# Loads of the first block over two DMA queues in another order, and a swap of two matmul groups, in a fused state-space and feed-forward kernel

## The chip, the cores and the metric

The kernel runs on one core of a Trainium2 chip. The core has five engines that run at once and meet through semaphores: TensorE (PE, matmuls; PEld is its weight load), VectorE (DVE), ScalarE (ACT), GpSimd (POOL) and SyncE (SP). The last one only issues DMAs here. ACT can issue DMAs too, on a queue of its own. The metric is device time in microseconds, and it is better when smaller.

## The reference

The input x has 2048 tokens of 512 features in bfloat16. It is normalised, and the output is x plus two branches of the normalised xn:

```python
xn = _layernorm(x, axis=-1)
return x + _A_ref(xn, Lambda_re, ..., Dskip) + _B_ref(xn, w_gate, w_up, w_down)

# A: a diagonal complex recurrence over the tokens
dt = exp(log_dt);  Lam_bar = exp(dt * Lam);  B_bar = ((Lam_bar - 1) / Lam)[:, None] * Bmat
h = Lam_bar * h + (xn @ B_bar.T)[t]                # for each token t
y = 2 * (h @ Cmat.T).real + xn * Dskip
# B: a gated feed-forward layer, 512 -> 1376 -> 512
(_gelu(xn @ w_gate) * (xn @ w_up)) @ w_down
```

The three vectors log_dt, Lambda_re and Lambda_im have 512 entries each; w_gate and w_up are 512 x 1376.

## The kernel before

**Tiling.** The tokens are cut into four blocks of 512, and a block into four token tiles of 128 rows: X[0] to X[15], 128 KB each. The feed-forward width is cut into 11 tiles of 128 columns (the last has 96). The contraction over 512 features goes in four steps of 128, called k = 0 to 3 here ("step 3" is k = 3).

**The first block.** Blocks 1 to 3 are normalised first and then multiplied. Block 0 starts before its statistics are known. Its token tiles are only centred (the mean is subtracted: lines 956 to 968 for tiles 0 and 1, line 951 for tiles 2 and 3), transposed by TensorE (`cent_T`, L684), evicted from PSUM by ACT (L689), and multiplied with the weights; the scale 1/sigma comes in when the sums are evicted (`GT_evac`, L721 and L724). `GT_k` (L701) is one matmul of contraction step k for token tile j and width part u: 256 columns wide when it takes gate or up alone, 512 when it takes both. `ks(k, j, [w])` issues the two parts u = 0, 1; w = 0 is gate, w = 1 is up. So the early matmuls can begin as soon as one token tile and 128 rows of w_gate are there. Line 936 keeps TensorE busy until then. After the early groups `GT_mm` (L712) does what is left of the first seven width tiles of block 0.

**The loads.** Each DMA is an operation of the queue that issues it. SP issues X[0]; then for k = 0 to 3 rows 128k to 128k+127 of the first 512 columns of w_gate and then of w_up (`ld_wk`, L488, 128 KB each), with X[3] ahead of k = 3; then the middle 384 columns of both (chunk 1, `ld_w`, L493), and the last 480 (chunk 2). ACT issues X[1], then the three parameter vectors as rows of a small tile PROW (`load_par`, L510), then X[2]. `tr_par` (L515) transposes PROW with a DMA on SP. From then on SP issues, in the order of the program: `TR(0)` (four DMA transposes of the normalised tiles of block 0, L736), the load of block 1, the transposing loads of B, the row Dskip, the load of block 2, `TR(1)`, and so on.

**What sets the order.** The operations are recorded with their reads and writes, from which the waits follow. Those of TensorE and SP run in the order in which they are recorded. Those of VectorE, ACT and POOL are put in order by a planner that reckons with costs of its own (a DMA holds its queue for 500 ns, unless told otherwise), save where `order_behind` ties one operation behind another; `ch` chains VectorE's early work in this way: mean and centring of tiles 0 and 1, statistics of tile 0, statistics and centring of tile 2, statistics of tile 1, statistics and centring of tile 3, then the normalising of tiles 0 and 1. `GATE["par"]` chains what ACT issues, and ties the mean of tile 1 (`mean1`, L956, on ACT) behind the last of it.

**Behind the first block** TensorE does the rest of the feed-forward layer of block 0 (`GU`, L843 and L817), the input products of the recurrence of blocks 0 and 1 (`BU`, L749; BU(1) begins with the first two token tiles of block 1, so with the first two transposes of TR(1)), then `GU`, `BU` and the down product with the state product (`DN`, L885) block by block. VectorE runs the recurrence (L774 to L803).

Of the kernel before, what the change touches and what calls it, by code (L numbers as in the profile page):

```python
# [361 lines left out]
def d_act(n, ptr=0): return 190.0 + 0.833 * n + 90.0 * ptr  # L362
# [3 lines left out]
def build(nc, ins, out):  # L366
    with ExitStack() as es:
        E = es.enter_context
        S = Sched(nc, es)
# [9 lines left out]
        WG = A.alloc("WG", [KD, F], BF16)  # L379
        WU = A.alloc("WU", [KD, F], BF16)  # L380
# [4 lines left out]
        WGc = [Buf("WGc%d" % i, "sbx", 10 * i, 10 * i + 1) for i in range(KD + 2)]  # L385
        WUc = [Buf("WUc%d" % i, "sbx", 100 + 10 * i, 101 + 10 * i) for i in range(KD + 2)]
# [34 lines left out]
        PROW = A.alloc("PROW", [128], BF16)  # L421
        PROW16 = Buf("PROW16", "sb", PROW.lo, PROW.hi, PROW.ap[0:16, :])
        PROWq = [Buf("PROW%d" % q, "prow", q, q + 1) for q in range(3)]
# [46 lines left out]
        GATE = {"before_gelu": [], "nh": 0}  # L470
        SCR = A.alloc("SCR", [1], F32)
        half = V(lambda e: e.memset(HALF.ap, 0.5), D_TINY, [], [HALF], "half")
# [10 lines left out]
                X_all.ap[:, 4 * b:4 * b + 4, :], x2[512 * b:512 * (b + 1), :].rearrange("(j p) d -> p j d", p=128)),  # L483
                512 * 1024, writes=X[4 * b:4 * b + 4], tag="ld_x%d" % b)

        def ld_wk(W, Wc, src, k):
            f0, f1 = FC[0]
            return S.dma(lambda e: e.dma_start(W.ap[:, k, f0:f1], src[128 * k:128 * (k + 1), f0:f1]),  # L488
                         256 * (f1 - f0), writes=[Wc[k]], tag="ld_w")

        def ld_w(W, Wc, src, n):
            f0, f1 = FC[n]
            return S.dma(lambda e: e.dma_start(W.ap[:, :, f0:f1], src[:, f0:f1].rearrange("(k p) f -> p k f", p=128)),  # L493
                         1024 * (f1 - f0), writes=[Wc[KD + n - 1]], tag="ld_w")

        def ld_x0(j, queue="sync", after=()):
            return S.dma(lambda e, j=j: e.dma_start(X[j].ap, x2[128 * j:128 * (j + 1), :]), 128 * 1024, writes=[X[j]], tag="ld_x0", queue=queue, after=after)  # L497
        ld_x0(0)
        GATE["par"] = S.order_behind(ld_x0(1, "scalar", [wrm]), GATE["table"])
        for k in range(KD):  # L500
            if k == 3:
                ld_x0(k)
            ld_wk(WG, WGc, ins["B_w_gate"], k)
            ld_wk(WU, WUc, ins["B_w_up"], k)
        ld_w(WG, WGc, ins["B_w_gate"], 1)
        ld_w(WU, WUc, ins["B_w_up"], 1)

        def load_par():
            for q, nm in enumerate(("A_log_dt", "A_Lambda_re", "A_Lambda_im")):
                GATE["par"] = S.order_behind(S.dma(lambda e, q=q, nm=nm: e.dma_start(PROW.ap[4 * q:4 * q + 4, :], ins[nm].rearrange("(s p) -> s p", p=128)),  # L510
                      1024, writes=[PROWq[q]], tag="ld_" + nm, queue="scalar", after=[half]), GATE["par"])
            GATE["par"] = S.order_behind(ld_x0(2, "scalar"), GATE["par"])

        def tr_par():
            S.dma(lambda e: e.dma_start_transpose(PAR.ap.rearrange("p q t -> p (q t)").unsqueeze(1), PROW16.ap), 4096,  # L515
# [162 lines left out]
        def cent_T(j, k0, k1, bank):  # L678
            pt = PS[bank].bitcast(BF16)[:, 0:128 * (k1 - k0)]

            def f(e):
                ins_ = None
                for k in range(k0, k1):
                    ins_ = e.transpose(pt[:, 128 * (k - k0):128 * (k - k0 + 1)], XN[j].ap[:, 128 * k:128 * (k + 1)], IDN.ap)  # L684
                return ins_
            PE(f, 56.0 * (k1 - k0), [XNp[j][k0 > 0] if j < 2 else XN[j], IDN], [BANK[bank]], "T0")
            dst, src = XC_all.ap[:, k0:k1, 128 * j:128 * (j + 1)], pt.rearrange("p (q t) -> p q t", t=128)
            w = XCs[j] if k1 - k0 == KD else [XCs[j][k0 > 0]]
            GATE["evTA"] = ACT(lambda e: e.activation(dst, src, ACTF.Copy), d_act(128 * (k1 - k0)), [BANK[bank]], w, "evT")  # L689
# [6 lines left out]
        def GT_k(k, j, u, ws, first=False):  # L696
            f0, f1 = FR[u]
            w = f1 - f0
            bank = acc(j, u)
            dst = PS[bank][:, w * ws[0]:w * (ws[-1] + 1)].rearrange("p (w f) -> p w f", w=len(ws))  # L700
            PE(lambda e: e.matmul(dst, XCd(j, k), WGU[:, ws[0]:ws[-1] + 1, k, f0:f1], start=first, stop=k == KD - 1, skip_group_check=True),  # L701
               d_pe([w * len(ws)]), [(WGc, WUc)[w_][k] for w_ in ws] + [XCs[j][k > 0]] + ([] if first else [BANK[bank]]), [BANK[bank]], "GK")
# [247 lines left out]
        def sub(j):  # L950
            return V(lambda e: e.tensor_scalar(XN[j].ap, X[j].ap, MVt[0][j].ap[:, 0:1], None, ALU.subtract),
                     d_dve_ts4x(512), [X[j], MVt[0][j]], [XN[j]], "sub")
        load_par()
        load_W()
        tr_par()
# [17 lines left out]
        def ks(k, j, w_, first=False):  # L973
            for u in range(2):
                GT_k(k, j, u, w_, first)
        cent_T(1, 0, 1, 6)
        ks(0, 0, [0], True)
        cent_T(1, 1, 4, 7)
        ks(0, 0, [1])
        ks(0, 1, [0], True)  # L980
        ks(0, 1, [1])
        ch(*stats(0, 0))
        for w_ in range(2):
# [75 lines left out]
def bass_parallel_sum__ssm_conv_s5__geglu_ffn__prompt_kernel(  # L1059
    nc: bass.Bass,  # L1060
    A_x: bass.AP,
    A_Lambda_re: bass.AP,
    A_Lambda_im: bass.AP,
    A_B_re: bass.AP,
    A_B_im: bass.AP,
    A_C_re: bass.AP,
    A_C_im: bass.AP,
    A_log_dt: bass.AP,
    A_Dskip: bass.AP,
    B_x: bass.AP,  # L1070
    B_w_gate: bass.AP,
    B_w_up: bass.AP,
    B_w_down: bass.AP,
    out: bass.AP,
):
    ins = {
        "A_x": A_x, "A_Lambda_re": A_Lambda_re, "A_Lambda_im": A_Lambda_im,
        "A_B_re": A_B_re, "A_B_im": A_B_im, "A_C_re": A_C_re, "A_C_im": A_C_im,
        "A_log_dt": A_log_dt, "A_Dskip": A_Dskip,
        "B_w_gate": B_w_gate, "B_w_up": B_w_up, "B_w_down": B_w_down,  # L1080
    }
    build(nc, ins, out)
# [28 lines left out]
```

## Time and profile before

| what | value |
|---|---|
| time, median of 3 runs | 177.05 us (176.91 to 177.43) |
| profiled execution | 177.26 us |
| its span | 175.9 us |
| busy: PE, DVE, ACT, POOL | 172.8, 159.7, 95.8, 10.7 us |
| granted TensorE clock | 1.00 |
| HBM read, written | 6.46 MB, 2.10 MB |

The span is what the profiler records, from the first instruction to the last; the profiled execution's time is 1.36 us longer. The loads of the start, from the trace (issue, and landing, which is issue plus the time to landing), in us from the start of the span:

| load | queue | issue | landing |
|---|---|---|---|
| X[0] | SP | 0.74 | 2.84 |
| X[1] | ACT | 1.00 | 3.2 |
| gate 0, up 0 | SP | 1.20, 1.66 | 3.6, 4.56 |
| gate 1, up 1 | SP | 2.13, 2.60 | 5.43, 6.27 |
| X[2] | ACT | 2.66 | 6.06 |
| gate 2, up 2 | SP | 3.08, 3.56 | 6.48, 7.16 |
| X[3] | SP | 4.03 | 7.5 |
| gate 3, up 3 | SP | 4.50, 4.98 | 8.1, 8.78 |
| chunk 1: gate, up | SP | 5.47, 5.95 | 10.27, 11.95 |
| chunk 2: gate, up | SP | 6.50, 7.04 | 13.3, 14.6 |
| parameter transpose | SP | 7.82 | 15.0 |

The three rows were issued by ACT at 1.42, 2.03 and 2.32; their landing is not in the trace.

### The profile page before, as it was taken

The numbers are of one execution on the slowest core, as the hardware profiler recorded it, in microseconds if no ns is written. First come the engines' busy times: TensorE is split into PE (matmuls) and PEld (weight loads), VectorE is DVE, ScalarE is ACT, GpSimd is POOL, SyncE is SP. The second block draws the span as 40 slices with busy tenths as digits, with TensorE's granted clock in tenths as the row PEclk, the third lists the DMA queues.
The fourth block names the chain that finished last, engine by engine and source line by source line (L and its number), as shares of the span: only waits on it lengthen the run. The fifth ranks groups of instructions, "written<-read, shape, count | busy, mean of one in ns | idle before, by whom it ended". The sixth has DMA issues, their size and how long they took to land.

```text
span 175.9 us, 2549 instructions
## 1 busy us (share of the span) xinstructions
PE 172.8 (98%) x903; PEld 85.4 (49%) x903; DVE 159.7 (91%) x279; ACT 95.8 (54%) x187; POOL 10.7 (6%) x24
## 2 busy tenths in 40 slices
PE   7999999999999999999999999999999999999995
PEld 2645664744544444444644444444464444444454
DVE  6797999987999989889899999989999899999941
ACT  5367668999766899383676793000667970000000
POOL 3132120211000000002200000000000000000000
DMA  5999989975899000002015000002004000000311
GB/s 144 281 322 154 216 136 203 174 132 114 162 270 270 11 0 2 0 30 75 18 33 112 5 0 4 0 0 89 30 0 34 0 0 0 0 0 4 119 62 60
DMA packets 32421, 14.36 MB, mean 82 GB/s; under 512 B 23737, under 2 KB 32409, under 8 KB 32409
## 3 DMA queue, kind: packets, MB, share of 16 engines
q1 hardware_dynamic: 31952, 13.84, 36.9%
q10 hardware_dynamic: 456, 0.36, 0.6%
q8 instruction: 7, 0.11, 0.3%
q14 instruction: 6, 0.04, 0.1%
HBM read 6.46 MB, written 2.10 MB: 49 GB/s over the span
## 4 chain that ended last, share of the span: by engine, by line
PE 95%; DMA 2%; SPq 1%; issue 0%; DVE 0%
PE PS L885 37%; PE PS L843 32%; PE PS L749 16%; PE PS L712 4%; PE PS L817 3%; PE PS L701 2%; DMA arena<-in_B_w_up_dram 2%; SPq L488 1%; PE PS L684 0%; SPq L497 0%; DVE arena L903 0%
## 5 line engine op out<-in xcount | busy, mean ns | idle before, releaser
L885 PE MATMUL PS<-arena 128*128 128x512 bf16 (+3 forms) x323 | 66.2, 366 | 0.0
L843 PE MATMUL PS<-arena 128*128 128x512 bf16 (+1 forms) x272 | 58.1, 373 | 0.0
L885 PEld LDWEIGHTS PS<-arena 128*128 128x128 bf16 (+1 forms) x323 | 30.8, 98 | 35.2
L843 PEld LDWEIGHTS PS<-arena 128*128 128x128 bf16 x272 | 26.5, 98 | 29.5
L787 DVE TENSOR_TENSOR_SCAN arena<-arena 128x512 bf16<-128x512 f32 x32 | 38.9, 1256 | 0.0
L859 ACT ACTIVATE arena<-PS 128x512 bf16<-128x512 f32 x33 | 19.8, 599 | 26.2 <-DVE arena L903 16.7
L749 PE MATMUL PS<-arena 128*128 128x512 bf16 (+1 forms) x144 | 28.3, 355 | 0.1
L863 ACT ACTIVATE arena<-PS 128x512 bf16<-128x512 f32 x33 | 19.8, 599 | 5.4 <-PE PS L843 5.4
L749 PEld LDWEIGHTS PS<-arena 128*128 128x128 bf16 x144 | 14.0, 98 | 13.7 <-DMA arena<-arena 0.6
L877 ACT ACTIVATE PS<-arena 128x512 f32<-128x512 bf16 (+2 forms) x17 | 9.6, 582 | 19.7 <-DVE arena L903 19.0
L758 ACT ACTIVATE arena<-PS 128x512 bf16<-128x512 f32 x32 | 17.6, 597 | 1.6 <-PE PS L749 1.6
L903 DVE TENSOR_TENSOR arena<-PS,arena 128x512 bf16<-128x512 f32 (+2 forms) x17 | 10.9, 654 | 6.4 <-PE PS L885 6.4
L865 DVE TENSOR_TENSOR arena<-arena 128x512 bf16<-128x512 bf16 x33 | 13.2, 419 | 2.1 <-ACT arena L863 2.0
L776 DVE TENSOR_TENSOR arena<-arena 128x4096 bf16<-128x4096 bf16 (+1 forms) x5 | 9.2, 1859 | 0.4 <-ACT arena L611 0.4
L799 DVE TENSOR_TENSOR arena<-arena 128x4096 bf16<-128x4096 bf16 x4 | 9.2, 2291 | 0.1
L774 DVE TENSOR_TENSOR arena<-arena 128x4096 bf16<-128x4096 bf16 (+1 forms) x5 | 9.2, 1861 | 0.0
L800 DVE TENSOR_TENSOR arena<-arena 128x4096 bf16<-128x4096 bf16 x4 | 9.1, 2287 | 0.0
L615 DVE BATCH_NORM_STATS2 arena<-arena 128x6 f32<-128x512 bf16 x12 | 7.8, 685 | 0.9 <-DMA arena<-in_A_x_dram 0.7
L721 ACT ACTIVATE arena<-PS,arena 128x256 bf16<-128x256 f32 (+1 forms) x16 | 6.5, 450 | 3.3 <-DVE arena L621 1.5
L712 PE MATMUL PS<-arena 128*128 128x512 bf16 (+1 forms) x40 | 7.1, 336 | 0.0
L701 PE MATMUL PS<-arena 128*128 128x256 bf16 (+1 forms) x36 | 6.2, 308 | 0.2 <-DMA arena<-in_B_w_up_dram 0.2
L724 DVE SCALAR_TENSOR_TENSOR arena<-PS,arena 128x256 bf16<-128x256 f32 (+1 forms) x16 | 6.2, 444 | 0.0
(95 smaller groups left out, 124.2 us busy)
## 6 DMA issues: line engine op xcount, KB each, us to landing
out_dram<-arena SPq DMA_DIRECT2D x15, 128.0 KB, 1.7
arena<-in_A_x_dram SPq DMA_DIRECT2D x3, 512.0 KB, 6.3
arena<-in_B_w_down_dram SPq DMA_DIRECT2D x1, 1280.0 KB, 8.8
arena<-in_B_w_gate_dram SPq DMA_DIRECT2D x4, 128.0 KB, 3.4
arena<-in_B_w_up_dram SPq DMA_DIRECT2D x4, 128.0 KB, 3.6
arena<-in_B_w_gate_dram SPq DMA_DIRECT2D x1, 480.0 KB, 6.8
arena<-in_B_w_up_dram SPq DMA_DIRECT2D x1, 480.0 KB, 7.6
arena<-arena SPq DMA_TRANSPOSE x25, 3.3
```

Source lines behind the costliest of these rows:

```text
L701: PE(lambda e: e.matmul(dst, XCd(j, k), WGU[:, ws[0]:ws[-1] + 1, k, f0:f1], start=first, stop=k == KD - 1, skip_group_check=True), d_pe([w ...
L712: ins_ = e.matmul(dst, XCd(j, k), WGU[:, :, k, f0:f1], start=(k == 0), stop=(k == KD - 1))
L749: ins_ = e.matmul(PS[bank][:, 128 * j0:128 * j1], BBT[c][dk].ap[:, 128 * s:128 * (s + 1)], XNT[b].ap[:, dk, 128 * j0:128 * j1], start=(dk ...
L758: GATE["evBu"] = ACT(lambda e, bank=bank, k3=k3, s=s, c=c: e.activation(SSc[k3][s][c].ap, PS[bank][:, :], ACTF.Copy), d_act(512), [BANK[ba ...
L787: V(lambda e, g=g, rb=rb, init=init: e.tensor_tensor_scan(g.ap, rb, g.ap, init, ALU.mult, ALU.add), d_dve_scan(512), [g, PA[RRr]] + ([CARc ...
L843: ins_ = e.matmul(PS[bank][0:m, c0:c1], W.ap[:, dk, 128 * ft:128 * ft + m], XNT[b].ap[:, dk, c0:c1], start=(dk == 0), stop=(dk == KD - 1))
L859: GATE["last_gelu"] = ACT(lambda e, bg=bg, kk=kk, m=m: e.activation(GG[kk].ap[0:m, :], PS[bg][0:m, :], ACTF.Gelu_apprx_tanh), d_act(512), ...
L863: ACT(lambda e, bu=bu, kk=kk, m=m: e.activation(UPB[kk].ap[0:m, :], PS[bu][0:m, :], ACTF.Copy), d_act(512), [BANK[bu]], [UPB[kk]], "evU")
L865: V(lambda e, kk=kk, m=m, ft=ft, k2=k2: e.tensor_tensor(HTt[k2][ft].ap[0:m, :], GG[kk].ap[0:m, :], UPB[kk].ap[0:m, :], ALU.mult), d_dve_tt ...
L877: ACT(lambda e: e.activation(PS[bank][:, c0:c1], X[tt].ap[:, c0:c1], ACTF.Copy), d_act(c1 - c0), [X[tt]], [BANK[bank]], "seed")
L885: ins_ = e.matmul(PS[bank][:, c0:c1], l_[:, 128 * j:128 * (j + 1)], r_[:, c0:c1], start=False, stop=last and n == len(ops) - 1, skip_group ...
L903: V(lambda e: e.tensor_tensor(OUTB[ko].ap[:, c0:c1], PS[bank][:, c0:c1], XD[tt].ap[:, c0:c1], ALU.add), d_dve_1x(c1 - c0), [BANK[bank], XD ...
```

## The change

The up rows of steps 0, 1 and 2 go from SP's queue to ACT's. X[2] stands behind the up rows of step 1 on ACT's queue, ahead of those of step 2. The three parameter rows go from ACT's queue to SP's, behind the up rows of step 3 and ahead of chunk 1; SP still issues chunk 1, chunk 2 and the parameter transpose in this order. `mean1` on ACT is now tied behind the up rows of step 2. In TensorE's order the gate matmuls of tile 1 in step 0 go ahead of the up matmuls of tile 0.

```diff
-        def ld_wk(W, Wc, src, k):
+        def ld_wk(W, Wc, src, k, queue="sync"):
             f0, f1 = FC[0]
             return S.dma(lambda e: e.dma_start(W.ap[:, k, f0:f1], src[128 * k:128 * (k + 1), f0:f1]),
-                         256 * (f1 - f0), writes=[Wc[k]], tag="ld_w")
+                         256 * (f1 - f0), writes=[Wc[k]], tag="ld_w", queue=queue)
...
             if k == 3:
                 ld_x0(k)
             ld_wk(WG, WGc, ins["B_w_gate"], k)
-            ld_wk(WU, WUc, ins["B_w_up"], k)
-        ld_w(WG, WGc, ins["B_w_gate"], 1)
-        ld_w(WU, WUc, ins["B_w_up"], 1)
+            if k < 3:
+                GATE["par"] = S.order_behind(ld_wk(WU, WUc, ins["B_w_up"], k, "scalar"), GATE["par"])
+            else:
+                ld_wk(WU, WUc, ins["B_w_up"], k)
+            if k == 1:
+                GATE["par"] = S.order_behind(ld_x0(2, "scalar"), GATE["par"])
 
         def load_par():
             for q, nm in enumerate(("A_log_dt", "A_Lambda_re", "A_Lambda_im")):
-                GATE["par"] = S.order_behind(S.dma(lambda e, q=q, nm=nm: e.dma_start(PROW.ap[4 * q:4 * q + 4, :], ins[nm].rearrange("(s p) -> s p", p=128)),
-                      1024, writes=[PROWq[q]], tag="ld_" + nm, queue="scalar", after=[half]), GATE["par"])
-            GATE["par"] = S.order_behind(ld_x0(2, "scalar"), GATE["par"])
+                S.dma(lambda e, q=q, nm=nm: e.dma_start(PROW.ap[4 * q:4 * q + 4, :], ins[nm].rearrange("(s p) -> s p", p=128)),
+                      1024, writes=[PROWq[q]], tag="ld_" + nm)
+            ld_w(WG, WGc, ins["B_w_gate"], 1)
+            ld_w(WU, WUc, ins["B_w_up"], 1)
...
         cent_T(1, 1, 4, 7)
+        ks(0, 1, [0], True)
         ks(0, 0, [1])
-        ks(0, 1, [0], True)
         ks(0, 1, [1])
```

## The prediction

> **What bounds the kernel now.** I read four views, from the whole to the spot. First the page: busy times (its part 1) and the chain that ended last (its part 4).
>
> ```profile
> PE 172.8 (98%) x903; PEld 85.4 (49%) x903; DVE 159.7 (91%) x279; ACT 95.8 (54%) x187; POOL 10.7 (6%) x24
> ...
> PE 95%; DMA 2%; SPq 1%; issue 0%; DVE 0%
> ```
>
> TensorE is the bound, with 95% of the chain. What is not matmul lies at the start, so the second view is that chain in order of time (start us, length, what).
>
> ```profile
> 2.60 3.67 DMA arena<-in_B_w_up_dram
> 6.28 0.05 issue
> 6.32 1.26 PE PS L701 x10
> ...
> 31.52 0.12 issue
> 31.64 7.11 PE PS L749 x48
> ```
>
> TensorE waits at two places that end last. One is at 6.3: the load of up rows, step 1, issued at 2.60 by SP, lands at 6.27. The matmul before it started at 5.84 and costs 0.11 (the spacing of the 256-wide ones), so 6.32 - 5.95 = 0.37 us are lost. The other is at 31.6, where BU(1) begins; the matmul before it started at 31.14 and costs 0.22, so 0.28 is lost. From 31.64 to the end TensorE runs without a gap. The third view, the timeline, says what feeds the two places (start us, length, engine, line, what; in brackets the idle time before and its releaser).
>
> ```profile
> 2.66 0.36 ACTq L497 DMA_DIRECT2D arena<-in_A_x_dram  x1
> 6.11 0.69 DVE L615 BATCH_NORM_STATS2 arena<-arena 128x6 f32<-128x512 bf16 x1 [0.74 <-DMA arena<-in_A_x_dram]
> 7.06 0.35 DVE L951 TENSOR_SCALAR arena<-arena 128x512 bf16<-128x512 bf16 x1
> 7.46 0.23 PEld L684 LDWEIGHTS PS<-arena 128*128 128x128 bf16 x4 [0.16 <-DVE arena L951]
> 7.82 1.99 SPq L515 DMA_TRANSPOSE arena<-arena  x1
> 9.82 0.73 DVE L634 TENSOR_SCALAR arena<-arena 128x512 bf16<-128x512 bf16 x2
> 10.27 5.15 SPq L736 DMA_TRANSPOSE arena<-arena  x4
> 24.17 6.34 SPq L736 DMA_TRANSPOSE arena<-arena  x4
> 31.61 6.64 PEld L749 LDWEIGHTS PS<-arena 128*128 128x128 bf16 x48 [0.58 <-DMA arena<-arena]
> ```
>
> Token tile 2 (X2) is issued by ACT at 2.66 and lands 3.4 later, at 6.06. VectorE has waited 0.74 for it, and then works without a gap (statistics, L951, statistics of two more tiles) until it normalises token tile 0 at 9.82. That lets SP start TR(0) at 10.27, and from there SP issues one DMA behind the other (loads, the transposes of B) to TR(1) at 24.17. The second transpose of TR(1), issued at 26.62, lands 4.9 later, at 31.5, and TensorE stands at 31.36 waiting for it. So the wait at 6.3 lies on the path of TensorE alone, and a second path, X2 - VectorE - TR(0) - SP - TR(1), arrives 0.28 later at 31.6. **What ends last there is the landing of X2, not that of up.** A microsecond that TensorE wins before 31.6 shows in the time only as far as this path moves too.
>
> The fourth view is the DMA queues, in a table by stages (engines' busy times, granted clock, DMA share, GB/s) and in the window 4.5 to 5.0 (q1 is SP's queue, q10 is ACT's).
>
> ```profile
> 2.00:3.00 1.00, 1.00 (x4) 0.43 (x3) 0.45 (x2) 0.23 (x2) 0.37 (x2) 1.00 0.97 329
> 3.00:4.50 1.50, 1.36 (x10) 0.43 (x9) 1.24 (x7) 1.21 (x4) 0.00 (x0) 1.00 0.75 197
> 4.50:6.00 1.50, 1.50 (x16) 1.14 (x15) 0.83 (x3) 0.92 (x3) 0.00 (x0) 1.00 1.00 338
> ...
> q10 hardware_dynamic: 97, 0.09, 54.0%
> q1 hardware_dynamic: 90, 0.09, 49.1%
> ```
>
> The engines are full at 330 GB/s, but between 3.0 and 4.5 they get work for only 197: SP issues one 128 KB load each 0.47 us, and ACT issues three rows of 1 KB. When both queues hold data, each gets half.
>
> **The change, part by part.** SP loses three up loads and gains three rows; ACT issues X1, up 0, up 1, X2, up 2 instead of X1, three rows, X2. An ACT issue of 128 KB takes 0.37 and 0.04 between, so I expect them at 1.00, 1.42, 1.83, 2.24, 2.65. SP issues X0, gate 0, 1, 2, X3, gate 3, up 3 by 4.0, then the three rows, the four chunks, and the parameter transpose (L515).
>
> *Up of step 1.* On ACT's queue at half of 330 GB/s a load takes 0.79. X1 had all packets by 3.0, so up 0 is through at 3.8, up 1 at 4.6, X2 at 5.35, up 2 at 6.15. From last packet to landing the rows of before show 0.25 (X1) to 0.5. Up 1 lands at 4.9 to 5.1, before its use at 5.95. The wait of 0.37 goes.
>
> *TensorE's order.* Gate of tile 1 now needs the eviction of that tile's first transpose, which ended at 4.93; the matmul in that place started at 4.86. Cost 0.07 to 0.31 (the nearest wait for an operand there, 0.31 at 4.37); I take 0.12, a semaphore's delay behind 4.93. Mean1 on ACT stands behind five issues, which end at 3.03 as before, or at 3.30 if each takes the 0.43 of SP's: 0 to 0.1. All of it is covered: without its wait TensorE would reach the transposes of tile 2 at 7.43 - 0.37 + 0.12 + 0.1 = 7.28 at worst, and L951 frees them at 7.41. If that cover were gone, 0.2 would stay before 11 us and be swallowed at 31.6, where TensorE has 0.28.
>
> *X2, the term that counts.* Issued 0.42 earlier, but behind two more loads on its own queue. Below: every 0.1 that it lands earlier moves VectorE, TR(0) and TR(1) by 0.1, down to 5.36, where VectorE is free: at most a gain of 0.74 - 0.04 = 0.70. Above: it is the eighth load by issue; the eighth to land before was at 6.48 and the ninth at 7.16, so a loss of 0.42 to 1.10. I take the queue sum, 5.35, and the 0.6 that X2 itself showed between its bulk (5.4 at the latest) and landing: 5.95, a gain of 0.1. It lies nearest because it uses the measured half share.
>
> *Rows and the parameter transpose.* An issue of a row took 0.27 to 0.57 on ACT, so SP is at L515 between 7.4 and 8.2, as before (7.82) within 0.4. It also waits for the rows, which now go behind 12 loads: 12 x 131 KB at 330 GB/s, from 2.0 on, are through at 6.8, and the landing is 0.25 to 0.5 later, say 7.2. From below nothing is won (L515's result was waited for at 15.1 by POOL behind all loads). From above: the twelfth load landed at 8.78 before; L515 would then start at 8.9, end at 10.9, and TR(0) begin 0.66 late. I take nothing, since TR(0) has 0.46 behind L515's end at 9.81.
>
> *The rest.* X3 comes earlier by 1.4 in issue and was used 0.84 after landing: nothing. Chunk 1 landed at 10.27 and 11.95 and is used at 12.73: up to 0.4 later costs nothing. PROW's clearing by POOL ended at 1.22, long before SP issues the rows.
>
> **Sum.** -0.1 at 31.6, and TensorE, which stood there at 31.36, is in time. The profiled execution took 177.26 (span 175.9 and 1.36 around it), 0.21 above the median of 177.05. So 177.16 for it, and 176.95 for the median.
>
> The Trainium skill ("DMA: Bandwidth & Descriptors", section "Issuing engines are not separate DMA queues") says that starting DMAs from several engines saves only the sequencer's time, as all run on the same 16 engines. The trace agrees for 4.5 to 6.0 (338 GB/s, share 1.00) and shows sequencer time to be saved from 3.0 to 4.5 (share 0.75). By the rule alone X2 would win what the idle quarter of 1.5 us gives and lose its extra load ahead, near nothing. Its section "Queues, rings and completion order" has each engine take turns between queues, which 54.0% and 49.1% bear out.
>
> **The rivals.**
> *X2 lands early (faster).* For it: the idle quarter of 3.0 to 4.5 is worth 0.25 x 1.5 = 0.38, and X2 is issued 0.42 earlier; with its old 3.4 to landing it is there at 5.64, with X0's 2.1 before VectorE is free. If it lands before 5.53, the time falls by 0.53 to 0.70: 176.4. Against it: two more loads ahead of it, and that L515 must start by 7.7 (it holds SP for 1.99, and TR(0) would have to begin at 9.74).
> *X2 lands late (slower).* ACT's queue carries three weight loads, and when SP's queue gets more than half, X2 falls from the seventh to the ninth place. It decides from a landing of 6.6; between that and 7.16 it costs 0.53 to 1.10: 177.85. For it: gate 2, issued after X2 before, landed only 0.42 after it. Against: equal shares. The skill's rule named above speaks for this one.
> *Rows land late (slower).* A new wait of SP at L515, as worked out: from rows at 8.7 on; 177.05 + 0.66 = 177.7. For it: the rows now stand behind 0.9 MB in their own queue; against: SP's old weight queue is three loads shorter there.
> *The wait is only renamed* is my forecast itself: up no longer holds TensorE, L951 does.
>
> **How the numbers follow.** The bound of what a measurement tells is 0.3%, 0.53 us. Renamed wait, 176.95, between 176.6 and 177.45: 0.43. X2 early: 0.27. X2 late: 0.17. Rows late: 0.13. So faster 0.27, same 0.43, slower 0.30. The range reaches from 176.4 to 177.9: it leaves out X2 at its floor and the upper part of its delay.
>
> **What would show it.** Right: no wait for in_B_w_up at L701; a wait for L951 of some 0.3 ahead of tile 2's transposes; L615 still waiting for in_A_x until about 6.0; L515 near 7.8; TR(0) near 10.2; BU(1) near 31.5 and dense matmuls behind it. Wrong: L615's wait ending before 5.5 or after 6.6, L515 after 8.4, or a gap of TensorE behind 31.6 that was not there, such as VectorE or ACT taking their work in another order, which no row of before prices.

## The result, and the profile after

The changed kernel takes 178.01 us (median of six runs, 177.73 to 178.16). The kernel before took 176.98 beside it (176.71 to 177.43). The ratio is 1.005, with a 95% interval of 1.0037 to 1.0063: **slower by about 0.9 us**, beyond the 0.3% that a measurement can tell. The prediction was 176.95, no change, so it was wrong in its sign and by 1.06 us; 178.01 lies just above its upper end, 177.9. The profiled execution took 177.82 (span 176.5, and 1.3 outside it, much as before). One run of all those below (180.07, of the kernel with X2 first on ACT's queue) was slower than the other runs of its kernel by over 1.5%, and is in no ratio here.

The page after, its busy times and its chain by engine:

```profile
PE 173.3 (98%) x903; PEld 86.1 (49%) x903; DVE 159.7 (90%) x279; ACT 95.3 (54%) x187; POOL 12.9 (7%) x24
...
PE 94%; DMA 3%; DVE 1%; ACTq 0%; ACT 0%; issue 0%
```

TensorE is still the bound. What changed is the start of the chain. In order of time (start us, length, what):

```profile
2.38 4.58 DMA arena<-in_A_x_dram
...
6.98 0.71 DVE arena L619
...
8.34 0.40 PE PS L688 x4
...
25.48 13.85 PE PS L753 x80
```

The load of up rows, step 1, has left the chain. In its place stands X2, issued at 2.38 and landed 4.58 later, then VectorE's statistics and centring of that tile, then TensorE's transposes of it at 8.34 (7.47 before). There is no break at BU(1) any more: L753 runs through. (Lines of the new code are four higher than those of before.) The timeline of the changed kernel gives the waits (start us, length, engine, line, what, and in brackets the idle time before and its releaser):

```profile
6.98 0.69 DVE L619 BATCH_NORM_STATS2 arena<-arena 128x6 f32<-128x512 bf16 x1 [1.48 <-DMA arena<-in_A_x_dram]
7.93 0.35 DVE L955 TENSOR_SCALAR arena<-arena 128x512 bf16<-128x512 bf16 x1
8.34 0.40 PE L688 MATMUL PS<-arena 128*128 128x128 bf16 x4 [0.49 <-DVE arena L955]
8.79 1.19 SPq L519 DMA_TRANSPOSE arena<-arena  x1
11.14 5.15 SPq L740 DMA_TRANSPOSE arena<-arena  x4
25.23 5.25 SPq L740 DMA_TRANSPOSE arena<-arena  x4
```

VectorE now waits 1.48 for X2 (0.74 before), and TensorE 0.49 for the centring of that tile. The landings show what the new order did (us, issue plus time to landing; the view gives that time in tenths, so each is good to 0.05, and X2's 6.98 is the 6.96 of the texts put down before the runs):

| load | before | after |
|---|---|---|
| X0, X1 | 2.84, 3.20 | 2.94, 3.30 |
| gate 0, up 0 | 3.60, 4.56 | 3.99, 4.81 |
| gate 1, up 1 | 5.43, 6.27 | 5.86, 6.30 |
| X2 | 6.06 | 6.98 |
| gate 2, up 2 | 6.48, 7.16 | 6.52, 7.37 |
| X3, gate 3, up 3 | 7.53, 8.10, 8.78 | 7.20, 7.67, 8.05 |

The twelve loads together are through 0.7 earlier (8.05 against 8.78), but the same first eight (to gate 2 before, to X2 after) end 0.5 later (6.98 against 6.48). Up 1, for which a second queue was opened, landed at the same time. X2 came 0.9 later; what came earlier, by 0.3 to 0.7, are X3, gate 3 and up 3. Landings scatter from one execution to the next, but the two orders stay apart: in five traces with the order of loads of before X2 landed at 5.5 to 6.1, in four with the changed order at 6.3 to 7.0.

How full the engines were, by stages of the kernel before (stage, busy us and instructions of PE, PEld, DVE, ACT, POOL, granted clock, DMA share, GB/s):

```profile
3.00:5.00 2.00, 1.86 (x16) 0.87 (x15) 1.74 (x7) 1.65 (x5) 0.00 (x0) 1.00 0.82 236
5.00:6.50 1.50, 1.29 (x13) 0.86 (x11) 0.72 (x3) 0.49 (x1) 0.00 (x0) 1.00 0.94 300
```

and of the changed kernel:

```profile
3.00:5.00 2.00, 1.95 (x11) 0.77 (x10) 1.67 (x7) 1.47 (x5) 0.00 (x0) 1.00 0.90 225
5.00:6.50 1.50, 1.50 (x15) 1.32 (x13) 0.47 (x2) 0.65 (x2) 0.00 (x0) 1.00 1.06 367
```

From 3 to 5 us the rate is no higher with two loaded queues than with one (225 against 236; 208 to 268 in the four traces with the changed order, 230 to 272 in the five with that of before), though the engines' busy share is (0.90 against 0.82). The gain, 367 against 300 (330 to 375 against 285 to 308), comes after 5 us and goes to loads of both queues alike, also to those that nobody waits for yet.

### The profile page after: what moved, and what is told of

Read it like the earlier page. It is cut to its first block, busy times and chain, and to the rows that moved or that the text cites. A ratio compares the mean times of both kernels' runs of the same rounds, so it can differ in the third digit from the quotient of the medians.

```text
span 176.5 us, 2549 instructions
## 1 busy us (share of the span) xinstructions
PE 173.3 (98%) x903; PEld 86.1 (49%) x903; DVE 159.7 (90%) x279; ACT 95.3 (54%) x187; POOL 12.9 (7%) x24
## 4 chain that ended last, share of the span: by engine, by line
PE 94%; DMA 3%; DVE 1%; ACTq 0%; ACT 0%; issue 0%
PE PS L889 37%; PE PS L847 32%; PE PS L753 16%; PE PS L716 4%; PE PS L821 3%; DMA arena<-in_A_x_dram 3%; PE PS L705 2%; ACTq L488 0%; PE PS L688 0%; DVE arena L619 0%; ACT L474 0%; DVE arena L955 0%; DVE arena L907 0%; DVE arena L620 0%
## 5 line engine op out<-in xcount | busy, mean ns | idle before, releaser
L753 PE MATMUL PS<-arena 128*128 128x512 bf16 (+1 forms) x144 | 28.2, 355 | 0.0
L753 PEld LDWEIGHTS PS<-arena 128*128 128x128 bf16 x144 | 14.1, 98 | 13.3
L705 PE MATMUL PS<-arena 128*128 128x256 bf16 (+1 forms) x36 | 6.4, 321 | 0.0
```

The source lines that it names most:

```text
L753: ins_ = e.matmul(PS[bank][:, 128 * j0:128 * j1], BBT[c][dk].ap[:, 128 * s:128 * (s + 1)], XNT[b].ap[:, dk, 128 * j0:128 * j1], start=(dk ...
```

## The experiments

The theory at the start (P in the texts put down before the runs): X2's late landing alone is the loss. The rivals: the swap in TensorE's order (S), two loaded queues that slow every load (Q), up 0 and up 1, and contention by what SP sends ahead. One number ties the traces together. T(2), the start of the transposes of token tile 2 on TensorE, and the span differ by 168.0 to 168.3 in the after trace and all twelve below (by 168.4 in the first trace of before, of which more later). So what moves T(2) moves the time, and nothing behind it counts. Where X2 sets T(2), it does so 1.33 to 1.41 after landing: statistics 0.69, aggregation, centring 0.35.

| kernel | ratio to before (95%) | X2 lands | T(2) |
|---|---|---|---|
| after | 1.0050 (1.0037 to 1.0063) | 6.98 | 8.34 |
| after, again | 1.0042 (1.0026 to 1.0058) | 6.79 | 8.15 |
| after, swap undone | 1.0040 (1.0025 to 1.0055) | 6.27 | 8.10 |
| after, X2 first on ACT | 1.0039 (1.0024 to 1.0054) | 4.62 | 7.95 |
| before, X2 late on SP | 1.0043 (1.0031 to 1.0055) | 6.85 | 8.20 |
| before, X2 early | 1.0004 (0.9992 to 1.0016) | 5.22 | 8.07 |
| after, tile 2 from X1 | 1.0016 (1.0003 to 1.0030) | 6.87 | 7.55 |
| after, X2 on SP | 1.0010 (0.9998 to 1.0023) | 6.32 | 7.65 |
| before and swap | 1.0010 (0.9999 to 1.0021) | 5.65 | 7.49 |
| after, SP held | 1.0028 (1.0017 to 1.0038) | 6.48 | 7.87 |
| before, again | 0.9995 (0.9982 to 1.0008) | 5.96 | 7.32 |
| before, tile 2 from X1 | 1.0003 (0.9991 to 1.0016) | not waited for | 8.14 |
| before, up 1 from up 0 | 1.0004 (0.9992 to 1.0015) | waited for until 6.17 | 7.80 |

Landing and T(2) are those of one profiled execution, the ratios those of all runs; the two can differ, for a reason shown in the last section.

**The swap undone.** In the changed kernel:

```diff
-        ks(0, 1, [0], True)
         ks(0, 0, [1])
+        ks(0, 1, [0], True)
         ks(0, 1, [1])
```

> The changed kernel with the swap of the two matmul groups undone; the loads stay as changed. Theory P (the place of X2): the loss comes from X2 landing at 6.96 instead of 6.06, which holds VectorE's statistics and through L955 the transposes of tile 2 on TensorE. P expects X2 near 6.96 again and the time of the changed kernel, 178.0 within 0.2. Rival S (the swap): gate of tile 1 ahead of up of tile 0 delays TensorE; S expects about 177.0. Rival Q (two queues slow each other down, every load with them): 178.0 as well.

Measured: 177.66 (177.13 to 178.14). Most of the loss stays, so the swap is not what it hangs on, though the time is a little below the 177.8 to 178.2 that P expected. X2 landed earlier in this trace, at 6.27, and T(2) was set by TensorE, which ran slowly for long (last section); so this trace alone doesn't say what the median is made of.

**X2 first on ACT's queue.** In the changed kernel:

```diff
+            if k == 0:
+                GATE["par"] = S.order_behind(ld_x0(2, "scalar"), GATE["par"])
...
-            if k == 1:
-                GATE["par"] = S.order_behind(ld_x0(2, "scalar"), GATE["par"])
```

> The changed kernel with X2 moved two places forward on ACT's queue: X1, X2, up 0, up 1, up 2. P expects X2 to land by about 5.2, the wait of VectorE for it to be gone by 5.4, and the time to fall by 0.5 to 1.0 against the changed kernel (177.0 to 177.5); up 1 takes the place in which X2 landed at 6.96, so TensorE should now wait for up 1 until about 6.9. S and Q expect the time of the changed kernel, 178.0, as the swap and the two loaded queues are still there.

Measured: five runs from 177.32 to 178.08, median 177.45, mean 177.64. X2 landed at 4.62 and nobody waited for it, and yet the mean is only 0.33 below that of the changed kernel (177.96; the standard error of the difference is 0.17) and still 0.4% above the kernel before, where P expected a fall of 0.5 to 1.0: a miss. Up 0 moved to 5.60 and up 1 to 6.69. The timeline of this kernel, TensorE:

```profile
5.34 2.77 PE L705 MATMUL PS<-arena 128*128 128x256 bf16 x20
5.67 2.16 PEld L705 LDWEIGHTS PS<-arena 128*128 128x128 bf16 x18 [0.18 <-DMA arena<-in_B_w_up_dram]
7.95 0.39 PE L688 MATMUL PS<-arena 128*128 128x128 bf16 x4
```

A weight load waited 0.18 for up 0, but the matmuls ran from 5.34 to T(2) without a break, at first slowly (last section). So in this execution no load held T(2). Had TensorE been at full speed early, up 1 would have: in the first trace of before up 1 landed at 6.27 and TensorE was through with what stands ahead of T(2) at 7.43, so with up 1 at 6.69 an estimate of T(2) is 7.85. That whichever of X2, up 0 and up 1 stands last pays fits this, but is argued and not shown.

**X2 early in the kernel before.** Its line in `load_par` moved ahead of the three rows:

```diff
+            GATE["par"] = S.order_behind(ld_x0(2, "scalar"), GATE["par"])
             for q, nm in enumerate(("A_log_dt", "A_Lambda_re", "A_Lambda_im")):
...
-            GATE["par"] = S.order_behind(ld_x0(2, "scalar"), GATE["par"])
```

> The kernel before with X2 issued ahead of the three rows on ACT's queue (1.42 instead of 2.66); SP's loads and TensorE's order are untouched. P expects X2 near 4.7, VectorE's chain 0.7 earlier, and the time lower by no more than 0.3, since TensorE still waits for up 1 until about 6.3 and reaches the transposes of tile 2 at 7.4: 176.7 to 177.0. If the second path of the prediction (TR(0) sets TR(1)) is right, the gain is 0.4 (SP is held by L515 until 9.8); S and Q expect 177.0.

Measured: 176.95 (176.67 to 177.56), the kernel before to 0.1%. X2 landed 0.84 earlier than in the first trace, and up 0 went from 4.56 to 5.46. The timeline, TensorE's weight loads:

```profile
5.50 2.45 PEld L701 LDWEIGHTS PS<-arena 128*128 128x128 bf16 x20 [0.38 <-DMA arena<-in_B_w_up_dram]
```

**X2 late in the kernel before.** Neither the swap nor weights on ACT's queue; X2 alone goes to SP's, behind gate 2:

```diff
             ld_wk(WG, WGc, ins["B_w_gate"], k)
+            if k == 2:
+                ld_x0(2)
...
-            GATE["par"] = S.order_behind(ld_x0(2, "scalar"), GATE["par"])
```

> The kernel before with X2 taken off ACT's queue and put on SP's, behind gate 2 and ahead of up 2; no weight load on ACT's queue, no swap, rows on ACT's queue as before. P expects X2 to land near 7.1, the transposes of tile 2 near 8.5, and a loss of 0.7 to 1.0 as in the changed kernel: 177.7 to 178.0, although up 1 lands no later than before. S and Q expect 177.0, as neither the swap nor a second loaded queue is there.

Measured: 177.76 (177.46 to 177.84). The timeline of this kernel:

```profile
6.84 0.69 DVE L616 BATCH_NORM_STATS2 arena<-arena 128x6 f32<-128x512 bf16 x1 [1.47 <-DMA arena<-in_A_x_dram]
8.20 0.40 PE L685 MATMUL PS<-arena 128*128 128x128 bf16 x4 [0.60 <-DVE arena L952]
```

The same two waits as in the changed kernel, of nearly the same size (1.47 and 0.60 against 1.48 and 0.49), and 0.0043 of the 0.0050. A late X2 is enough to make the loss.

**The wait for X2 taken out of the changed kernel.** All loads stay as they are, but statistics and centring of tile 2 read X1, which is there long before:

```diff
+            src = 1 if tt == 2 else tt
...
+            src = 1 if j == 2 else j
...
```

(Left out: the lines below each, in which X[src] stands in place of X[tt] and X[j].)

> The changed kernel, every load in its place, but the statistics and the centring of token tile 2 read X1 instead of X2, so that part of the output is computed from the wrong tile: VectorE's wait for X2 is gone and the traffic of the DMA engines is untouched. P (VectorE's wait for X2 holds the transposes of tile 2 and all of TensorE behind them) expects L619 of tile 2 right behind that of tile 0, near 5.5, and the time down by 0.4 to 1.0 from the changed kernel, to 177.0 to 177.6; what is left over the kernel before is what up 1 and up 2 and TensorE's slow start allow. If rows, parameter transpose or the swap made the loss, it stays at 178.0.

Measured: 177.20 (176.84 to 177.84), with the changed kernel again beside it at 177.71. The timeline without the wait:

```profile
5.41 0.66 DVE L620 BATCH_NORM_STATS2 arena<-arena 128x6 f32<-128x512 bf16 x1
7.32 0.11 PEld L706 LDWEIGHTS PS<-arena 128*128 128x128 bf16 x2 [0.31 <-DMA arena<-in_B_w_up_dram]
7.55 0.39 PE L689 MATMUL PS<-arena 128*128 128x128 bf16 x4
```

X2 landed as late as ever, at 6.87, with the same traffic. 0.51 of the 0.77 that the changed kernel lost in this comparison goes with the wait (the means differ by 0.46, with a standard error of 0.15 worked out from 12 and 10 runs). So a late X2 is also needed for the larger part of the loss. The 0.26 left is small, but the interval of this kernel's ratio, 1.0003 to 1.0030, lies above 1. The trace shows what comes next: TensorE waits 0.31 for up 2, now the last load of ACT's queue, and T(2) at 7.55 is 0.1 to 0.2 later than in the two traces of before (7.47 and 7.32). That up 2 is the rest fits; no run tested it.

**The changed kernel again**, without an edit:

> The changed kernel once more, unchanged, for a second trace and for the same chip as the others here. P expects X2 to land between 6.3 and 7.1 and 177.7 to 178.1. Were X2's landing of 6.96 in the first trace an exception, it would lie near 6.2 here with the time still at 178.0, and P would fall.

Measured: 177.71 (177.18 to 178.24). Its timeline:

```profile
6.80 0.69 DVE L619 BATCH_NORM_STATS2 arena<-arena 128x6 f32<-128x512 bf16 x1 [1.29 <-DMA arena<-in_A_x_dram]
8.15 0.40 PE L688 MATMUL PS<-arena 128*128 128x128 bf16 x4 [0.28 <-DVE arena L955]
```

The same wait ends last in a second execution.

**The swap alone**, in the kernel before:

```diff
+        ks(0, 1, [0], True)
         ks(0, 0, [1])
-        ks(0, 1, [0], True)
```

> The kernel before with only the swap of the two matmul groups. P expects no change, 177.0 within 0.2, as the wait for up 1 until 6.3 covers it. S (the swap costs) expects 177.3 to 177.5, the difference between the changed kernel and the one without the swap.

Measured: 177.14 (176.75 to 177.47), ratio 0.9999 to 1.0021. The swap costs between nothing and 0.2%.

**X2 on SP's queue behind gate 1**, in the changed kernel, so up 0, 1 and 2 stay on ACT's queue:

```diff
             if k == 1:
-                GATE["par"] = S.order_behind(ld_x0(2, "scalar"), GATE["par"])
+                ld_x0(2)
```

> The changed kernel with X2 on SP's queue behind gate 1, so that each queue carries four or five of the loads that are needed first and X2 is issued at 2.1. If P holds and X2 was late because it stood fourth on ACT's queue at half the rate while SP's half went to gate 2 and X3, X2 lands at 5.8 to 6.3 and the time is 177.0 to 177.5. If the two loaded queues themselves are the loss, whichever load stands where, it stays at 177.7 to 178.0.

Measured: 177.19 (176.94 to 177.58). X2 landed at 6.32, up 1 at 6.09:

```profile
6.30 0.69 DVE L619 BATCH_NORM_STATS2 arena<-arena 128x6 f32<-128x512 bf16 x1 [1.04 <-DMA arena<-in_A_x_dram]
7.65 0.40 PE L688 MATMUL PS<-arena 128*128 128x128 bf16 x4
```

Two loaded queues by themselves are not the loss; X2's place behind two up loads on the second one is. Nor are they a gain: this arrangement, the best of those tried, stands no better than the kernel before.

**SP held back.** In the changed kernel X3, gate 3, up 3 and all behind them wait until tile 0 is centred, so that SP doesn't send ahead what nobody needs yet:

```diff
             if k == 3:
-                ld_x0(k)
+                break
...
-        load_par()
-        load_W()
-        tr_par()
...
+        ld_x0(3, after=[tail_op[0]])
+        ld_wk(WG, WGc, ins["B_w_gate"], 3)
+        ld_wk(WU, WUc, ins["B_w_up"], 3)
+        load_par()
+        load_W()
+        tr_par()
```

> The changed kernel, but SP holds X3, gate 3, up 3 and all that follows until token tile 0 is centred (near 3.9), so that between 2.6 and 3.9 SP issues nothing; ACT's queue is as changed (X1, up 0, up 1, X2, up 2). Sharing theory (X2 and up are late because SP's queue, rid of the up loads, runs ahead with X3 and gate 3 and takes half of the engines): X2 lands at 5.9 to 6.3, up 2 by 6.7, and the time is 177.0 to 177.4. Rival (the fourth load of ACT's queue lands near 6.9 whatever SP does): X2 at 6.7 to 7.0, 177.7.

Measured: 177.51 (177.23 to 177.68). X2 landed at 6.48, between the two expectations; the timeline:

```profile
6.51 0.70 DVE L616 BATCH_NORM_STATS2 arena<-arena 128x6 f32<-128x512 bf16 x1 [1.02 <-DMA arena<-in_A_x_dram]
```

That is 0.31 and 0.50 earlier than in the two traces of the changed kernel, and the time is lower by 0.2 to 0.5. But the landings of one load order differ by as much between executions (6.27 with the swap undone, 6.98 with it). That sharing with SP's later loads is a part of the delay is supported and not settled.

**The kernel before again**, without an edit, for the stall at 31.6:

> The kernel before once more, for a second trace. The prediction read the wait at 31.6 for TR(1) as lasting; in the traces of the other kernels so far no such wait stands. If it belonged to that one execution, it is absent here, the span is 175.3 to 175.6, and the matmuls go on without a gap; if it belongs to the kernel, TensorE waits here for TR(1) again by 0.2 to 0.4.

Measured: 176.92 (176.64 to 177.54), span 175.5. Its timeline:

```profile
5.97 0.69 DVE L615 BATCH_NORM_STATS2 arena<-arena 128x6 f32<-128x512 bf16 x1 [0.69 <-DMA arena<-in_A_x_dram]
7.32 0.40 PE L684 MATMUL PS<-arena 128*128 128x128 bf16 x4
...
23.97 5.12 SPq L736 DMA_TRANSPOSE arena<-arena  x4
24.24 9.82 PEld L749 LDWEIGHTS PS<-arena 128*128 128x128 bf16 x59
```

The four issues of TR(1) took 5.12 here and 6.34 in the first trace, and TensorE's weight loads run through 31.6 with no wait in brackets. The stall of 0.28 belonged to that one execution; none of the other thirteen traces has it.

**The wait for X2 taken out of the kernel before**, by the same edit as above:

> The kernel before with the statistics and the centring of token tile 2 reading X1 instead of X2 (part of the output is computed from the wrong tile), no load moved. The prediction's reading (the landing of X2 ends last in the kernel before, not up) expects a gain of 0.3 to 0.5. The other reading (up 1 and the rest of TensorE's path end last) expects no more than 0.15.

Measured: 176.91 (176.64 to 177.56), ratio 0.9991 to 1.0016. Nothing is won: a miss of what the prediction's reading expected.

**The wait for up 1 taken out of the kernel before.** The up matmuls of step 1 read the rows of step 0:

```diff
+            kw = 0 if k == 1 and ws == [1] else k
-            PE(lambda e: e.matmul(dst, XCd(j, k), WGU[:, ws[0]:ws[-1] + 1, k, f0:f1], start=first, stop=k == KD - 1, skip_group_check=True),
-               d_pe([w * len(ws)]), [(WGc, WUc)[w_][k] for w_ in ws] + [XCs[j][k > 0]] + ([] if first else [BANK[bank]]), [BANK[bank]], "GK")
+            PE(lambda e: e.matmul(dst, XCd(j, k), WGU[:, ws[0]:ws[-1] + 1, kw, f0:f1], start=first, stop=k == KD - 1, skip_group_check=True),
+               d_pe([w * len(ws)]), [(WGc, WUc)[w_][kw] for w_ in ws] + [XCs[j][k > 0]] + ([] if first else [BANK[bank]]), [BANK[bank]], "GK")
```

> The kernel before with the up matmuls of step 1 of tiles 0 and 1 reading the up rows of step 0, which have landed (part of the output is computed from the wrong rows), no load moved: the wait for up 1 is gone. The prediction's reading expects nothing, since X2 then holds the transposes of tile 2 at 7.4 as before. The other reading expects a gain of 0.15 to 0.35.

Measured: 177.14 (176.74 to 177.53), ratio 0.9992 to 1.0015. Nothing is won here either. With the last two runs and the early X2, three single waits of the kernel before were taken away or moved, and each of them was worth nothing. This fits that TensorE's own pace, the up rows and X2 end there at about the same time, so that a later one costs and an earlier one gains nothing; no run took two of them away at once.

## Why the prediction was wrong

**The step that failed first** is the landing of X2: "I take the queue sum, 5.35, and the 0.6 that X2 itself showed between its bulk (5.4 at the latest) and landing: 5.95, a gain of 0.1." It landed at 6.98, 6.87 and 6.79 in three traces of this load order, and at 6.27 in the fourth, with the swap undone. Against the first, two terms of that sum were too small.

- *The rate.* "On ACT's queue at half of 330 GB/s" held from 5 us on, where two loaded queues moved 367, not from 3. Between 3 and 5 they moved 225 GB/s, so ACT's half is 0.225 MB by 5.0. Up 0, up 1 and X2 are 0.393 MB; the other 0.168 at half of 367 takes 0.92, so X2's bulk is through at 5.92 and not at 5.35. That is 0.57 of the miss of 1.03. I had put the 197 GB/s of the early stage down to too few issues ("they get work for only 197"). With the issues of two queues it was 225 from 3 to 5, against 236 with one, at a higher busy share of the engines, so issuing was not what held it back. What does, the runs don't say.
- *The tail.* From bulk to landing X2 then took 1.06, not 0.6. By the same sum up 1 (0.262 MB) is through at 5.2 and landed at 6.30, again 1.1 later. This is no fixed delay behind the last packet: the last packet on ACT's queue, of up 2, started at 6.94, and up 2 landed only 0.48 later. The trace has sixteen updates of a load's semaphore, as many as the core has DMA engines. Those of X1 come within 0.17 us, from 3.10 to 3.27; those of X2 are spread over 1.39, from 5.57 to 6.96 (in the first trace of before over 0.96, from 5.13 to 6.09). A load has landed when the last of the sixteen has come, and a sum over the queue as a whole leaves their spread out. I had taken the spread of a less loaded queue.

The packets show the first term too small in all four traces, the second clearly so in two. ACT's queue had sent as many packets as X2 and the loads ahead of it have by 5.89, 6.03, 5.83 and 5.53 (after, after again, tile 2 from X1, swap undone; the landings are 6.98, 6.79, 6.87 and 6.27), each later than 5.35; from there to the landing it took about 1.1, 0.8, 1.0 and 0.7.

The same sum made "Up 1 lands at 4.9 to 5.1" wrong: it landed at 6.30, as before. The sentence "The wait of 0.37 goes" came out true in the profile, as there is no wait for up at L705, but not by an earlier load. TensorE reached those matmuls later.

**The rule that I weighed and did not follow.** The Trainium skill ("DMA: Bandwidth & Descriptors", section "Issuing engines are not separate DMA queues") says that starting DMAs from several engines saves only the sequencer's time. The rows agree, up 1 at 6.30 against 6.27 most plainly. I had it speak for the rival.

**The rival that happened** is "X2 lands late", given a chance of 0.17 and 177.85. Its point of decision (6.6) and its price (0.53 to 1.10) held: measured 0.77 to 1.03 with landings of 6.79 to 6.98, though by another path than the one that it was worked out on (below). Its mechanism held in part: X2 was late on a queue with weight loads, but it landed eighth and not ninth, and SP's queue didn't get more than half. Its argument against, "equal shares", was no argument: shares are near equal (51.2% and 49.1% in the window from 5.0 to 5.5), but an equal share of a queue with three more loads on it is late.

**The second path.** "A second path, X2 - VectorE - TR(0) - SP - TR(1), arrives 0.28 later at 31.6. What ends last there is the landing of X2" was read from a stall of one execution. It is not in the repeat. In the changed kernel TR(1) starts 1.06 later (25.23 against 24.17) and TensorE still doesn't wait for it, so that path has room. X2 does end last, but by the other way: L955 holds the transposes of tile 2 on TensorE. The stall also flatters the change in the two profiled executions: T(2) is 0.87 later, the span only 0.6 longer, and the 0.28 is the rest.

**"L951 frees them"** was the right wait at the wrong time: it took 0.49 and 0.28 in the two traces, where I had about 0.3, but ended at 8.34 and 8.15 and not at 7.4.

**The swap**, 0.12 and covered: the swap alone is between -0.01% and 0.21%. Nothing contradicts it.

**The rows.** I had L515 between 7.4 and 8.2 and called anything after 8.4 a sign of being wrong. It came at 8.79: SP waited 1.6 for the last row, which landed at 8.7 and not near 7.2. It cost nothing, as "TR(0) has 0.46 behind L515's end" became more, not less: L519 ended at 9.98 and TR(0) started at 11.14, held back by the late tile 2 on VectorE.

**The early X2** (0.27, 176.4): X2 at 5.22 in the kernel before gained nothing, and at 4.62 in the changed one left it 0.4% above the kernel before. "Every 0.1 that it lands earlier moves VectorE, TR(0) and TR(1) by 0.1" is right for VectorE and wrong for the time. TensorE's pace and up 0 or up 1 ending as late fits that, as said above.

## What to carry to other kernels

Where several loads are each needed just in time, opening a second queue doesn't bring one of them forward for nothing: list what lands when, and see which load takes the place that another gives up. Price a load's landing with the rate measured at that moment of the kernel, not with the best rate of a later stage, and add the spread between the DMA engines on a queue that is as full as it will be. And take a second trace of the same kernel before building a step on a stall of a few tenths of a microsecond: here it was not there the second time.

## What was not expected of the hardware

TensorE starts at half its speed and turns to full speed at a time that differs from one execution to the next. The timelines of the same kernel, the changed one, in its two traces; first:

```profile
4.62 0.61 PE L705 MATMUL PS<-arena 128*128 128x256 bf16 x2
5.02 0.53 PE L688 MATMUL PS<-arena 128*128 128x128 bf16 x3
```

and again:

```profile
4.62 0.38 PE L705 MATMUL PS<-arena 128*128 128x256 bf16 x2
4.83 0.33 PE L688 MATMUL PS<-arena 128*128 128x128 bf16 x3
```

The same five matmuls take 0.61 and 0.53 in one and 0.38 and 0.33 in the other. By the spacing of matmuls of 128 columns (0.107 against 0.056) the turn came between 3.6 and 6.8 us in the fourteen traces: at 3.7 and 4.8 in the two of the kernel before, at 6.8 in the kernel before with tile 2 from X1. The granted clock of the windows reads 1.00 throughout, so it doesn't show this. Turning late makes TensorE the last to arrive at T(2), as in five of the traces above, with T(2) at 7.80 to 8.14 although X2 was there in time or not waited for. That run with the turn at 6.8 took 177.49, where the median of its kernel is 176.91. It fits that the kernel before scatters over 176.3 to 177.6; that the turn is the whole of the scatter was not shown.

The Trainium skill ("TensorE: Matmul & The Clock Gate", Part 1) describes such a turn, after a window of 3.4 us that runs freely and doesn't begin with the kernel. The traces agree in the spread, 3.2 us between the earliest and the latest turn with the first matmul always at 0.77 to 0.78; the earliest turn, 2.8 us behind the first matmul, comes sooner than such a window is long.
